# Loading wq by halves of its rows, summing Q in load order, two filler matmuls, and a new order table

## The chip, the cores and the metric

The kernel runs on one core of a Trainium2 chip. The metric is the device time of one execution in microseconds (us), the median of several runs. Before the change it is 269.3 us (four runs, 269.09 to 270.72).

## What is computed

The reference mixes two branches of the same input x (2048 tokens x 512, bf16), token by token, with a gate:

```python
x = A_x
g = sigmoid((x * gate_w).sum(-1, keepdims=True))
a = infini_attention(x, wq, wk, wv, wo, beta)        # 32 heads of 16
b = (relu(x @ W_gate) * (x @ W_up)) @ W_down          # 512 -> 1792 -> 512
return g * a + (1 - g) * b
# attention, for each of 4 segments of 512 tokens:
#   o = gb * (phi(q) @ M) / (phi(q) @ z) + (1 - gb) * causal_softmax(q k' / 4) v
#   M += phi(k)' v ;  z += sum(phi(k))               # phi(t) = t + 1 if t > 0 else exp(t)
```

## The kernel before, in words

**Tiling.** The 2048 tokens are four segments of 512 (L). x is kept transposed (xT, four chunks of 128 features by 512 tokens). Every projection is a set of matmuls of 128x128 weights by 512 tokens: Q and K in four chunks of eight heads per segment (proj_q, proj_k), V in four token tiles (proj_v), gate and up of the feed-forward part in 14 chunks each (ffn_tasks), and the output in token tiles of 128 that sum the down projection and wo into the same PSUM bank (out_tile). Scores are packed four heads to the array's rows ("row" groups of 8 matmuls, L625, and the diagonal ones of 32, L638), probabilities times V four to its columns ("col" groups of 32, two per unit of eight heads, L697). PSUM is eight banks of 512 columns (pool "ps"), shared by all.

**Other engines.** ACT does exp of the scores (L646, four banks at once), exp for phi (L535) and relu (L847). DVE empties banks (QT L555, ktr L571, hT L853), makes the two masked copies of K (KT L574), phi (pkT, pqT, L530 and L531), transposes and normalises the attention output (T L728, cfr L736 and L738, och L733, oT L709) and sums x times gate_w (L433, reads xn, the natural rows of x). GpSimd masks the probabilities (L675). SP issues nearly all DMAs, in program order: loads (L299), the transposing loads of xT for segments 1 to 3 (load_xT, L306), xn of segments 1 to 3 (load_xn, L309), the transposing copies of pkT into pK (L587), Vm (L610), coefficients (coefs, cdr), and the stores of the output (L878).

**The order of the work.** The kernel does not leave the order to a scheduler of the compiler. Each piece of work is a task with an engine, an assumed duration, a key, dependencies and buffers that it needs and frees (plan.add). Plan.run plays the tasks through: on each engine the ready task of lowest key goes next, subject to free banks and buffers; then instructions are emitted in the order of the start times so found. The table SHIFT adds an amount to the key of single tasks, by the number of the task. LANDS gives the assumed landing time of each initial load, in ns. SP is assumed busy with these loads until 31,500 ns, and a load of xn to take 520 ns of SP and to land 3,500 later; a pK copy takes 1,200 and 2,000. None of these assumptions is a measured time of the chip; they only set the order. A wrong assumption shows as a wait at run time.

**The start.** Four 128-token tiles of x come in by SP and ACT queues (xn), followed on SP by wq in two halves of 256 columns, wk, wv, the first pieces of W_gate and W_up, and the rest. Six matmuls on a zeroed tile (heat, L888) keep PE busy while x is awaited. PE transposes the four tiles of x into xT of segment 0 (x0_tasks, flip, L510), the copies out of PSUM go by DVE and ACT (L516). In proj_q of segment 0 the first two chunks (those that lie in the first half of wq) are computed in two halves of 256 tokens, each as a sum over the four feature chunks; the other two chunks in one piece of 512 tokens.

Tensors of one pool are told apart by a number: four pkT buffers hold phi(k) until pK has been copied from them, and a fifth write to pkT waits for the first copy to land.

```python
got_q = [load_cols(nc.sync, wq_sb, A_wq, 256 * i, 256 * i + 256, "q" + "ab"[i])
         for i in range(2)]
```

```python
plan.add("SP", 520, KA(4 * seg - 4), lambda seg=seg: load_xn(seg), att["xn", seg - 1], 3500)
```

Of the kernel before, what the change touches and what calls it, by code (L numbers as in the profile page):

```python
# [12 lines left out]
P = 128  # L13
# [6 lines left out]
L = S // NSEG  # L20
F = 1792
NC = D // P
# [7 lines left out]
RH = 14  # L30

SHIFT = {
    43: -11292, 47: -42077, 60: 29780, 61: -29343, 78: -7855, 80: -28982, 81: 10949, 82: 54730,
    83: 61225, 85: 1523, 92: 60668, 99: 17134, 105: 23333, 108: 6042, 135: 68788, 155: 81196,
    171: -26874, 178: 28954, 203: 14280, 206: 25983, 212: 15078, 215: -1330, 218: -18032,
    221: -5316, 224: -4814, 230: 4174, 233: -3831, 239: 5098, 242: 32097, 245: 1369, 248: 1978,
    254: 346, 257: -3395, 260: -10949, 263: -6816, 266: 12793, 272: -2789, 275: -11469,
    283: -20102, 284: 10561, 299: 13751, 337: 44621, 342: 12310, 345: 10169, 354: -30001,
    356: -45046, 358: 80101, 368: -61348, 372: -4345, 373: -49237, 380: -41791, 389: 27518,
    391: 4652, 394: -20195, 395: -41145, 400: 33640, 401: 12661, 405: 14171, 414: 8957,  # L40
    420: 65824, 446: -24413, 476: 42115, 512: 24141, 533: 21455, 550: -7924, 553: -9644,
    555: -16953, 562: 1704, 565: -3083, 574: 10306, 577: -6358, 583: -18575, 586: 1273,
    589: -14836, 592: -5785, 595: -12158, 598: -6986, 601: -6263, 604: -2900, 610: -5726,
    613: -20978, 619: 12853, 631: -124737, 670: 51001, 671: 27573, 677: -73050, 681: 4127,
    695: -9393, 700: 6645, 709: 12451, 714: -3470, 737: -44032, 739: 33239, 743: 5687,
    746: -27812, 761: 17624, 777: 24417, 789: 46875, 813: -11642, 829: 49888, 844: -14954,
    862: 32683, 867: -2735, 873: 4060, 879: 1169, 882: 518, 888: 10427, 891: -5165, 897: -3609,
    900: -8372, 903: -10859, 906: -5138, 912: -7446, 915: -6121, 924: 1808, 927: 3218, 930: 4603,
    942: 3963, 945: 1904, 948: -2731, 975: 7041, 987: 40475, 1007: -59044, 1014: 8606,
    1022: 31523, 1025: 4449, 1030: 2648, 1047: -2009, 1052: 10394, 1058: 20655, 1064: 9096,  # L50
    1067: 9109, 1099: -58805, 1134: 19973, 1151: -15341, 1161: -24899, 1162: -66525,
    1185: -54718, 1191: -19721, 1197: 30339, 1203: -5307, 1206: -13430, 1209: 25922,
    1218: -21029, 1224: 86677, 1230: 1511, 1236: -18972, 1239: -22798, 1242: -9229, 1245: 8841,
    1248: 7291, 1251: 33147, 1257: -26262, 1260: -16305, 1263: -14082,
}


# [154 lines left out]
def kernel(  # L212
# [15 lines left out]
    nc = tc.nc  # L228
# [7 lines left out]
    plan = Plan()  # L236

    def sb(shape, dtype, name):
        return wpool.tile(shape, dtype, name=name)
# [6 lines left out]
    xT = [sb([P, NC, L], BF16, f"xT{i}") for i in range(3)]  # L246
    xn = sb([P, 4, D], BF16, "xn")
    wq_sb = sb([P, NC, D], BF16, "wq_sb")
# [35 lines left out]
    def bank(slot):  # L284
        return ps[:, slot.i * L:(slot.i + 1) * L]

    def work():
        return plan.one("ps", range(7, -1, -1))


    LANDS = dict(n0=3500, n1=3700, n2=4750, n3=4850, qa=5600, qb=6900, k=8800, v=10200, g0=11700,
                 u0=13500, gw=14100, be=14200, g1=15700, u1=19000, x1=21200, g2=22400, u2=23700,
                 g3=24800, u3=25900, d0=28500, d1=31100, o=32700, x2=35700)

    def arrival(name):
        return plan.add("in_" + name, 0.0, 0.0, None, lat=LANDS[name])

    def load(eng, dst, src, name):
        eng.dma_start(out=dst, in_=src)  # L299
        return arrival(name)  # L300

    def load_cols(eng, t, ap, c0, c1, name):
        return load(eng, t[:, :, c0:c1], ap.rearrange("(c p) n -> p c n", p=P)[:, :, c0:c1], name)
# [9 lines left out]
    got_x, got_n, got_g, got_u = {}, {}, {}, {}  # L313
# [5 lines left out]
    def load_wd(a, b, name):  # L319
# [2 lines left out]

    got_n[0] = [load(nc.scalar if t % 2 else nc.sync, xn[:, t, :], x[t * P:(t + 1) * P, :],
                     "n%d" % t) for t in range(4)]
    got_q = [load_cols(nc.sync, wq_sb, A_wq, 256 * i, 256 * i + 256, "q" + "ab"[i])
             for i in range(2)]
    got_k = load_cols(nc.sync, wk_sb, A_wk, 0, D, "k")
    got_v = load_cols(nc.sync, wv_sb, A_wv, 0, D, "v")
# [8 lines left out]
    junk = sb([P, L], BF16, "junk")  # L337
# [80 lines left out]
    PEL, DVL, ACL, POL = 230, 150, 165, 130  # L418
    att, prj, ffn, xread, x0_first = {}, {}, {}, [], []
    UNIT, AUNIT = 16000.0, 14800.0  # L420

    def K(unit, part=0.0):
        return unit * UNIT + part
# [57 lines left out]
    def matmuls(key, deps, sl, ops, start=True, stop=True, prev=None, width=L, need=(), chunk={}, at=0):  # L481
        n = len(ops)
        for k in range(0, n, GM):
            def emit(k=k):
                for q in range(k, min(k + GM, n)):
                    lhsT, rhs = ops[q]()
                    nc.tensor.matmul(bank(sl)[:, at:at + width], lhsT=lhsT, rhs=rhs,  # L487
                                     start=(start and q == 0), stop=(stop and q == n - 1))
            first = prev is None
            m = min(k + GM, n) - k  # L490
            t = plan.add("PE", 215.8 * width / L * m, key - (0 if first else CONT), emit,
                         list(deps) + [d for q in range(k, k + m) for d in chunk.get(q, ())],
                         PEL, need=[sl] + list(need) if first else ())
            if not first:
                t.deps.append((prev, 0.0))
            prev, deps = t, ()
        return prev
# [4 lines left out]
    def x0_tasks():  # L502
        got = []
        parts = [(0, 0, 4), (1, 0, 4), (2, 0, 4), (3, 0, 2), (3, 2, 4)]
        for n, (t, c0, c1) in enumerate(parts):
            sl = work()

            def flip(t=t, c0=c0, c1=c1, sl=sl):
                for c in range(c0, c1):
                    nc.tensor.transpose(bank(sl).bitcast(BF16)[:, c * P:(c + 1) * P],  # L510
                                        xn[:, t, c * P:(c + 1) * P], ident[:])
            a = plan.add("PE", 107.0 * (c1 - c0), K(-9) + n, flip, [got_n[0][t]], PEL, need=[sl])
            act = n in (1, 4)
            b = plan.add(
                "ACT" if act else "DVE", 60 + (0.83 if act else 0.56) * P * (c1 - c0),
                K(-9), lambda t=t, c0=c0, c1=c1, sl=sl, act=act: (  # L516
                    nc.scalar.copy if act else nc.vector.tensor_copy)(
                    xT[0][:, c0:c1, t * P:(t + 1) * P],
                    bank(sl).bitcast(BF16)[:, c0 * P:c1 * P].rearrange("p (c q) -> p c q", q=P)),
                [a], DVL, frees=[sl])  # L520
            got.append(b)
        x0_first.extend(got[0:2])
        return [got[0:4], got[0:3] + got[4:5]]

    def proj_mm(w, c, seg):
        return [lambda ci=ci: (w[:, ci, c * P:(c + 1) * P], xT[seg % 3][:, ci, :])
                for ci in range(NC)]
# [10 lines left out]
    def proj_q(seg, c):  # L538
        u, sl = 4 * seg + c, work()
        i = u % RQ  # L540
        key = K(4 * seg + c - 2 - (2 if seg else 0))
        war = [att.get(("pv", u - RQ)), att.get(("recall", u - RQ))]
        if seg == 0 and c < 2:
            a = None
            for h in range(2):
                a = matmuls(key + 20000 * (h - 1), [got_q[0]], sl, [
                    lambda ci=ci, h=h: (wq_sb[:, ci, c * P:(c + 1) * P],
                                        xT[0][:, ci, h * L // 2:(h + 1) * L // 2])
                    for ci in range(NC)], width=L // 2, at=h * L // 2, prev=a,
                    chunk={ci: got_x[0][ci // 2] if h else x0_first for ci in range(NC)})  # L550
        else:
            a = matmuls(key, [got_q[c // 2]] + war, sl, proj_mm(wq_sb, c, seg),
                        chunk={ci: got_x[seg][ci // 2] for ci in range(NC)})
        xread.append(a)
        prj["q", seg, c] = plan.add("DVE", 600, key - RQK, lambda: nc.vector.tensor_copy(  # L555
            QT[i][:], bank(sl)), [a], DVL, frees=[sl])
        if seg:
            es, b = phi_exp(key, lambda: QT[i][:], prj["q", seg, c])
            prj["pq", seg, c] = plan.add("DVE", 665, key + 500, lambda: phi(
                pqT[i][:], QT[i][:], ex1[es.i][:]), [b], DVL, frees=[es],  # L560
                lock=True)
# [321 lines left out]
    GM, CONT, QKP, PVP = 2, 10000.0, 1e6, 1e5  # L883
# [73 lines left out]
```

## Time and profile before

| what | value |
|---|---|
| median of four runs | 269.3 us (269.09, 269.26, 269.35, 270.72) |
| the profiled execution | 269.09 us |
| its span (first to last instruction) | 267.4 us |
| instructions in the profile | 7193 |
| first matmul on wq | at 5.90 us |
| last eviction (osr, L875) | 264.36 to 264.84 us |
| mean DMA rate | 77 GB/s, 20.52 MB in 32567 packets |
| packets under 512 B, under 2 KB | 15000, 31000 |
| granted TensorE clock | 1.00 throughout |

All times in the profile are microseconds from the start of the span, of one execution. PE is TensorE's matmuls, PEld its weight loads, DVE VectorE, ACT ScalarE, POOL GpSimd; SPq is SP's queue, that is, the issuing of DMAs. "L487" is a line of the kernel: it is the line of the matmul in the helper `matmuls`, so all projections share it, and they are told apart by their tiles (ps<-xT,wq_sb is Q). A matmul's recorded duration includes its way through the array and is longer than the step from one matmul to the next; where steps matter, they are taken from start to start. The chain of waits is the work that ended last, followed back from the last instruction. A DMA's landing is the last of its completion increments in the trace.

### The profile page before, as it was taken

To read this page: it belongs to the slowest core of one execution; us is meant where nothing else is said; L and a number is where in the kernel's file an instruction comes from. 1 tells how busy PE (TensorE), PEld (TensorE's weight loads), DVE (VectorE), ACT (ScalarE), POOL (GpSimd) and SP (SyncE) were. 2 spreads that over 40 slices of the span, in tenths; PEclk is the share of its full clock that TensorE was granted. 3 is DMA by queue.
4 is the path that set the end of the run, shared out by engine and by line. 5 is a ranking of instruction groups with operands and counts; after the bars stand their busy time and mean duration, and the time that the engine had idled before them with its cause. 6 is when DMAs were issued, how large, how long until landed. Compare 5 with 4: busy or idle time off the path is not lost.

```text
span 267.4 us, 7193 instructions
## 1 busy us (share of the span) xinstructions
PE 262.5 (98%) x3022; PEld 117.3 (44%) x3022; DVE 197.9 (74%) x455; ACT 182.7 (68%) x168; POOL 57.8 (22%) x146
## 2 busy tenths in 40 slices
PE   7999999999999999999999999999999999999995
PEld 4544444444444444443444444344444444444444
DVE  3898889999997798899699287477996566554412
ACT  3299859999977779897897857745988656243200
POOL 7032112313222231322223222201132302200000
PEclk9999999999999999999999999999999999999999
DMA  7999972132626112011601210000310210000011
GB/s 208 341 263 338 266 167 41 23 99 50 112 52 182 31 37 91 2 20 42 116 19 25 88 54 9 2 0 2 81 55 2 93 56 20 2 0 2 0 39 39
DMA packets 32567, 20.52 MB, mean 77 GB/s; under 512 B 15000, under 2 KB 31000, under 8 KB 32536
## 3 DMA queue, kind: packets, MB, share of 16 engines
q1 hardware_dynamic: 32248, 19.82, 28.1%
q8 instruction: 23, 0.38, 0.7%
q10 hardware_dynamic: 288, 0.26, 0.4%
q14 instruction: 8, 0.07, 0.1%
HBM read 13.21 MB, written 2.55 MB: 59 GB/s over the span
## 4 chain that ended last, share of the span: by engine, by line
PE 95%; DMA 3%; DVE 1%; SPq 0%; issue 0%
PE ps L487 77%; PE ps L625 8%; PE ps L697 7%; DMA wq_sb<-in_A_wq_dram 2%; DMA pK<-pkT 1%; PE ps L783 1%; PE ps L638 1%; PE ps L802 1%; SPq L299 0%; DVE T L728 0%; PE ps L753 0%; DVE osr L875 0%; DVE pkT L530 0%; PE ps L452 0%; DVE pkT L531 0%
## 5 line engine op out<-in xcount | busy, mean ns | idle before, releaser
L646 ACT ACTIVATE E<-ps 128x2048 bf16<-128x2048 f32 x64 | 120.1, 1877 | 27.4 <-PE ps L625 21.5
L675 POOL TENSOR_SCALAR_AFFINE_SELECT E<-E 128x256 bf16<-128x256 bf16 x128 | 53.0, 438 | 172.0 <-ACT E L646 172.0
L487 PE MATMUL ps<-xT,wg_sb 128*128 128x512 bf16 x224 | 58.0, 380 | 0.0
L487 PE MATMUL ps<-xT,wu_sb 128*128 128x512 bf16 x224 | 56.5, 380 | 0.0
L487 PE MATMUL ps<-wd_sb,hT 128*128 128x512 bf16 (+1 forms) x238 | 55.3, 368 | 0.0
L853 DVE TENSOR_TENSOR hT<-ps,rgr 128x512 bf16<-128x512 f32 x56 | 37.7, 686 | 20.5 <-ACT rgr L847 11.6
L847 ACT ACTIVATE rgr<-ps 128x512 bf16<-128x512 f32 x56 | 32.9, 600 | 20.4 <-PE ps L487 20.4
L487 PEld LDWEIGHTS <-wu_sb 128*128 128x128 bf16 x224 | 21.0, 98 | 26.1 <-issue 2.6
L487 PEld LDWEIGHTS <-hT 128*128 128x128 bf16 x238 | 21.6, 98 | 24.2 <-issue 3.8
L487 PEld LDWEIGHTS <-wg_sb 128*128 128x128 bf16 x224 | 20.3, 98 | 25.0 <-issue 3.2
L875 DVE TENSOR_SCALAR osr<-ps,ngcol 128x512 bf16<-128x512 f32 (+1 forms) x17 | 12.0, 707 | 20.1 <-PE ps L487 20.1
L728 DVE STREAM_TRANSPOSE T<-ps 128x512 f32<-128x512 f32 x32 | 21.1, 696 | 7.2 <-PE ps L697 6.5
L625 PE MATMUL ps<-QT,KT 32*128 32x320 bf16 (+3 forms) x512 | 25.4, 273 | 0.0
L697 PE MATMUL ps<-E,Vp 128*17 128x320 bf16 (+3 forms) x512 | 18.8, 274 | 0.0
L646 ACT ACTIVATE Em<-ps 128x2048 bf16<-128x2048 f32 x8 | 15.0, 1874 | 4.6 <-PE ps L638 4.6
L625 PEld LDWEIGHTS <-KT 32*128 32x128 bf16 x512 | 7.7, 92 | 23.0 <-issue 22.1
L487 PE MATMUL ps<-xT,wk_sb 128*128 128x512 bf16 x64 | 17.0, 381 | 0.4 <-DVE T L728 0.4
L487 PE MATMUL ps<-wv_sb,xT 128*128 128x512 bf16 x64 | 17.0, 380 | 0.0
L487 PE MATMUL ps<-wo_sb,oT 128*128 128x512 bf16 (+1 forms) x68 | 16.6, 367 | 0.0
L487 PE MATMUL ps<-xT,wq_sb 128*128 128x512 bf16 (+1 forms) x72 | 16.5, 356 | 0.1
L697 PEld LDWEIGHTS <-Vp 128*17 128x17 bf16 x512 | 8.0, 91 | 10.0 <-issue 4.7
L571 DVE CAST ktr<-ps 128x512 bf16<-128x512 f32 x16 | 11.0, 686 | 1.6 <-PE ps L487 1.3
(87 smaller groups left out, 231.9 us busy)
## 6 DMA issues: line engine op xcount, KB each, us to landing
cdr<-coefs SPq DMA_DIRECT2D x12, 256.0 KB
out_dram<-osr SPq DMA_DIRECT2D x15, 128.0 KB
wd_sb<-in_B_W_down_dram SPq DMA_DIRECT2D x2, 896.0 KB
xn<-in_A_x_dram SPq DMA_DIRECT2D x3, 512.0 KB
Vm<-Vp SPq DMA_DIRECT2D x8, 144.0 KB
wg_sb<-in_B_W_gate_dram SPq DMA_DIRECT2D x2, 512.0 KB
wu_sb<-in_B_W_up_dram SPq DMA_DIRECT2D x2, 512.0 KB
wg_sb<-in_B_W_gate_dram SPq DMA_DIRECT2D x2, 384.0 KB
```

Of the source, the lines that this page charges most:

```text
L487: nc.tensor.matmul(bank(sl)[:, at:at + width], lhsT=lhsT, rhs=rhs, start=(start and q == 0), stop=(stop and q == n - 1))
L571: d = plan.add("DVE", 600, key - RQK, lambda: nc.vector.tensor_copy(ktr[ks.i][:], bank(sl)), [a], DVL + 40, need=[ks], frees=[sl])
L625: nc.tensor.matmul(ps[:, j * L + o:j * L + o + L - q], lhsT=KT[i][rows, kb, 3 * r:3 * r + 2].rearrange("p h q -> p (h q)"), rhs=QT[i][rows ...
L638: nc.tensor.matmul(ps[:, o:o + HP], lhsT=KT[i][rows, kb, 2:4].rearrange("p h q -> p (h q)"), rhs=QT[i][rows, kb * P:kb * P + HP], start=Tr ...
L646: last_exp[0] = [plan.add("ACT", 66 + 4 * L / 1.2, key, lambda: nc.scalar.activation(dst, ps[:, 0:4 * L], ACT.Exp, scale=SCALE), [a] + war ...
L675: nc.gpsimd.affine_select(out=m[:, :, o:o + HP], in_=m[:, :, o:o + HP], compare_op=ALU.is_ge, fill=0.0, base=HP, pattern=[[0, 4], [1, HP]] ...
L697: nc.tensor.matmul(bank(sl)[32 * j:32 * j + HW, q:q + w], lhsT=(Vp[i] if n < 4 else Vm)[:, kb, r, 4 * c + j, 0:HW], rhs=rhs, start=(n == 0 ...
L728: done.append(plan.add("DVE", 633, key - RL, lambda r=r, sl=sl: nc.vector.transpose(T[ts.i][:, r], bank(sl)), [a] + done, 75 if r else 0, ...
L783: a = plan.add("PE", 216, key, lambda: nc.tensor.matmul(bank(sl), lhsT=mbd[i][:, c].rearrange("p j r e -> p (j r e)"), rhs=pqT[u % RQ][:], ...
L847: r = plan.add("ACT", 478, key - RL, lambda sl=gsl, rs=rs: nc.scalar.activation(rgr[rs.i][:], bank(sl), ACT.Relu), [g], ACL, frees=[gsl])
L853: nc.vector.tensor_tensor(hT[hs1.i][:], bank(sl), rgr[rs.i][:], ALU.mult)),
L875: b = plan.add("DVE", 95 + 1.12 * w, key - RL, lambda: nc.vector.tensor_scalar(osr[os.i][:, 0:w], bank(sl)[:, 0:w], ngcol[:, tt:tt + 1], N ...
```

## The change

Four edits. First, wq is loaded in two halves of its rows (feature chunks 0 and 1, then 2 and 3, all 512 columns) instead of two halves of its columns. Second, Q of segment 0 is summed in the order in which these arrive, for all four chunks: the first 256 tokens over feature chunks 0 and 1, the second 256 tokens over chunks 0 and 1, then all 512 tokens over chunks 2 and 3; the three parts are sums into the same bank. Third, two matmuls of 256 columns on the zeroed tile are put after the transposes of the second tile of x and after those of the last. Fourth, LANDS has new values and SHIFT is another table: some 150 entries before, an entry for nearly every task after; the numbers of the tasks change as well, since Q has more tasks. With that the order of instructions on PE, DVE, ACT and SP changes everywhere except in stretches. The counts of instructions stay the same but for the two filler matmuls (with their weight loads). In the new order xn of segment 1 stands second after Vm on SP, behind the first pK copy (before: third, behind two), and on DVE the first operation that reads it (L433) stands right behind the first two T transposes of segment 0.

```diff
 SHIFT = {
-    43: -11292, 47: -42077, 60: 29780, 61: -29343, 78: -7855, 80: -28982, 81: 10949, 82: 54730,
...
+    23: 127287, 24: 109748, 25: 61282, 26: -14683, 27: -105670, 28: 80312, 29: 20669, 31: 93713,
...
-    LANDS = dict(n0=3500, n1=3700, n2=4750, n3=4850, qa=5600, qb=6900, k=8800, v=10200, g0=11700,
-                 u0=13500, gw=14100, be=14200, g1=15700, u1=19000, x1=21200, g2=22400, u2=23700,
-                 g3=24800, u3=25900, d0=28500, d1=31100, o=32700, x2=35700)
+    LANDS = dict(n0=3500, n1=3700, n2=4750, n3=4850, qa=5750, qb=6500, k=8050, v=9550, g0=11100,
+                 u0=12900, gw=13500, be=13600, g1=15100, u1=18400, x1=20600, g2=21800, u2=23100,
+                 g3=24200, u3=25300, d0=27900, d1=30500, o=32100, x2=35100)
...
-    got_q = [load_cols(nc.sync, wq_sb, A_wq, 256 * i, 256 * i + 256, "q" + "ab"[i])
+    got_q = [load(nc.sync, wq_sb[:, 2 * i:2 * i + 2],
+                  A_wq.rearrange("(c p) n -> p c n", p=P)[:, 2 * i:2 * i + 2], "q" + "ab"[i])
              for i in range(2)]
...
             a = plan.add("PE", 107.0 * (c1 - c0), K(-9) + n, flip, [got_n[0][t]], PEL, need=[sl])
+            if n in (1, 4):
+                fs = work()
+                plan.add("PE", 213 if n == 1 else 110, K(-9) + n + 0.5, lambda fs=fs:
+                         nc.tensor.matmul(bank(fs)[:, 0:2 * P], lhsT=junk[:, 0:P],
+                                          rhs=junk[:, None, 0:P].to_broadcast([P, 2, P]),
+                                          start=True, stop=True), [(a, 0.0)], PEL, need=[fs], frees=[fs])
...
-        if seg == 0 and c < 2:
+        if seg == 0:
             a = None
-            for h in range(2):
-                a = matmuls(key + 20000 * (h - 1), [got_q[0]], sl, [
-                    lambda ci=ci, h=h: (wq_sb[:, ci, c * P:(c + 1) * P],
-                                        xT[0][:, ci, h * L // 2:(h + 1) * L // 2])
-                    for ci in range(NC)], width=L // 2, at=h * L // 2, prev=a,
-                    chunk={ci: got_x[0][ci // 2] if h else x0_first for ci in range(NC)})
+            parts = [(0, L // 2, 0, x0_first), (L // 2, L, 0, got_x[0][0]), (0, L, 2, got_x[0][1])]
+            for n, (l0, l1, c0, got) in enumerate(parts):
+                a = matmuls(key + 20000 * (n - 2) + CONT * (n > 0), [], sl, [
+                    lambda ci=ci, l0=l0, l1=l1: (wq_sb[:, ci, c * P:(c + 1) * P],
+                                                 xT[0][:, ci, l0:l1])
+                    for ci in (c0, c0 + 1)], start=(n == 0), stop=(n == 2), width=l1 - l0, at=l0,
+                    prev=a, chunk={0: got + [got_q[c0 // 2]]})
         else:
-            a = matmuls(key, [got_q[c // 2]] + war, sl, proj_mm(wq_sb, c, seg),
+            a = matmuls(key, list(got_q) + war, sl, proj_mm(wq_sb, c, seg),
                         chunk={ci: got_x[seg][ci // 2] for ci in range(NC)})
```

## The prediction

> **What bounds the kernel now.** I read the page's engine rows first, then the chain of waits, then the table of stretches, then the timeline of DVE and of SP's queue around the one place where TensorE stands still.
>
> ```profile
> PE 262.5 (98%) x3022; PEld 117.3 (44%) x3022; DVE 197.9 (74%) x455; ACT 182.7 (68%) x168; POOL 57.8 (22%) x146
> ```
>
> PE is busy all but 5 us of the span. The chain (start, length, what) says where those 5 us are:
>
> ```profile
> 1.75 4.11 DMA wq_sb<-in_A_wq_dram
> 5.90 6.67 PE ps L487 x38
> ...
> 32.79 3.14 DMA pK<-pkT
> 35.95 0.31 DVE pkT L530
> 36.31 0.31 issue
> 36.62 0.72 DVE T L728
> 37.38 1.45 PE ps L487 x6
> ...
> 264.36 0.48 DVE osr L875
> ```
>
> Three things are to be seen. The first Q matmul (5.90) is released by the first half of wq (landed at 5.85). After that the chain is PE, line after line, until 264.3; then one eviction and one store end the span. Only once does it leave PE: a transposing DMA of pK, issued by SP at 32.79, releases DVE's pkT write (it needs that pkT buffer back), the two T transposes queue behind it on DVE, and PE waits for the bank that the first T frees. Start to start, PE loses 0.60 us there (36.77 to 37.38). Elsewhere after 5.9 I find 0.10 at 25.1, 0.14 at 68.5 and 0.14 at 168.0, and a few hundredths.
>
> DVE is the next engine (us, then busy PE, PEld, DVE, ACT, POOL):
>
> ```profile
> 6.00:38.00 32.00, 31.57 (x285) 14.24 (x285) 27.05 (x73) 23.24 (x27) 6.64 (x14) 1.00 1.01 277
> 38.00:100.00 62.00, 61.97 (x840) 26.77 (x839) 56.71 (x143) 52.00 (x46) 16.54 (x40) 1.00 0.33 77
> ```
>
> From 38 to 100 us DVE has 5.3 us free in 62. Until 38 us the DMA engines are busy all the time (share 1.01).
>
> ```profile
> 23.80 7.39 SPq L306 DMA_TRANSPOSE xT<-in_A_x_dram  x1
> 31.32 1.37 SPq L610 DMA_DIRECT2D Vm<-Vp  x2
> 32.79 3.23 SPq L587 DMA_TRANSPOSE pK<-pkT  x2
> 36.12 0.54 SPq L309 DMA_DIRECT2D xn<-in_A_x_dram  x1
> 36.62 1.31 DVE L728 STREAM_TRANSPOSE T<-ps 128x512 f32<-128x512 f32 x2
> 38.46 0.68 DVE L571 CAST ktr<-ps 128x512 bf16<-128x512 f32 x1
> 40.72 0.68 DVE L433 SCALAR_TENSOR_TENSOR junk<-xn,gwb 128x512 bf16<-128x512 bf16 x1
> ```
>
> SP is held by the transposing load of segment 2's xT for 7.39 us, so all that stands behind it in SP's order is late. By the trace's completion records the first pK landed at 35.93, the second at 37.31, xn (the natural rows of segment 1, for the gate) at 40.30. DVE first reads xn at 40.72, just after.
>
> **What the Trainium skill says.** "TensorE: Matmul & The Clock Gate", section "Wait — 56ns, not 53.3ns?": start to start a warm matmul takes N / 2.4 GHz and about 2.5 ns; cold, N / 1.2 GHz. The trace agrees: 216 ns at 512 columns, 109 at 256; the transposes step by 107 ns until 4.57 and by 55 from 4.98, so the clock is already full at the first Q. "DMA: Bandwidth & Descriptors", section "Specifications": 512 B is the least piece for full rate. Column halves of wq have 512 B pieces, row halves 1 KB; so little is to be won, and the trace agrees: wq's second half (256 KB) lands 0.79 us after the first, 332 GB/s, against 512 KB of wv in 1.50 us, 350 GB/s. Same page, section "Queues, rings and completion order": on each DMA engine descriptors are consumed in the order of the ring. That bears on xn behind pK; the landings above are in order of issue.
>
> **The change, part by part.**
>
> *Row halves of wq, Q in load order.* Same bytes, same 72 wq matmuls (16 of 256 columns). From the rates above a half saves 256 KB / 332 GB/s - 256 KB / 350 GB/s = 0.04 us. The first Q starts at 5.9, perhaps 5.75: gain 0 to 0.15. In the built order PE needs the second half after 12 x 0.109 = 1.3 us (it lands 0.79 after the first) and wk after 2.39 us (12 + 2 of 0.109 and 4 of 0.216), that is at 8.29; wk landed at 8.11. wv is needed at 9.80, landed 9.61; gate's second piece at 15.41 (before: 24.5), landed 15.14. All margins are thin (0.1 to 0.3) but positive: 0, at worst 0.3 of stall.
>
> *Two fillers.* 0.109 us each warm, 0.213 cold. The first stands where PE is idle from 4.63 to 4.98 waiting for x, the second where it is idle from 5.62 to 5.90 waiting for wq. Both covered; if wq came early, the second would show 0.11.
>
> *None of that reaches the end.* The wait at 37.38 is set by SP and the DMA (7.39 us of xT, Vm, pK landing 35.93), not by PE. In the changed order SP's first four of these are the same, and so are DVE's pkT, T, T. Summing PE's matmuls with the durations above (score group 0.33 and 0.10 to enter it, PV pair 1.22), from the first Q to the matmul that waits for T both orders give 30.75 us. So a gain of 0.15, or a stall of up to 0.6, before 36.8 vanishes in this wait. Value taken: 0, the ends -0.1 (if the loads come earlier by two halves) and +0.1.
>
> *The new order (SHIFT, LANDS).* This is the larger part: almost every task's key changes. Three counts from the built orders. (1) Entries from full-array matmuls into score or PV groups: 79 before, 77 after, 0.098 us each (62 of them measured): -0.19. (2) Waits of PE on DVE or ACT whose releasing work begins with a matmul less than 1.55 us before: 23 before and 23 after (past 37 us). So close waits are as many; the small stalls (0.14, 0.14) I carry over unchanged, with -0.3 and +0.4 as ends. (3) Loads: from 76 to 98 us the two orders are nearly the same; near 68 the gate's small loads come earlier.
>
> One place differs for the worse. In SP's new order xn stands right behind the first pK, and in DVE's new order the first gate operation (L433, reads xn) stands right behind the two T, ahead of the cast of K (ktr); before, the cast came at once (38.46), the gate at 40.72. Working it out: SP is free for xn at 34.76 (32.79 and the first pK's issue, 1.93 by the trace). The one xn issued into an almost empty queue (54.03) landed 3.61 us later: 38.36 at the earliest. In this stretch xn landed 2.99 after the pK ahead of it (37.31 to 40.30): 35.93 + 2.99 = 38.92 at the latest by that row. I take 38.7. DVE ends T at 37.93 and waits to 38.75; the gate's pair takes 0.72, the cast 0.68, the signal 0.06: PE has the bank at 40.2. PE wants it 2.16 us after 37.38 (in the new order four wk, two wq, a score group with its entry, two wq: 8 x 0.216 + 0.43), at 39.54. Stall 0.67 (0.33 to 0.9). Queued behind on DVE: cfr, four KT, och, oT, then QT0, hT. By the same sums QT0 is ready at 43.2 (wanted at 43.3), the second hT at 45.0 (wanted at 44.9): another 0.15. DVE's later gate operations are the same number, so what is done early here is not owed later, but PE's loss is not given back: PE has no idle time.
>
> *Sum against the profiled execution* (269.09 us, its span 267.4 and 1.7 outside): 269.09 + 0.67 + 0.15 - 0.19 = 269.72. The median of the runs, 269.3, lies 0.2 above that execution: **269.9**.
>
> *Tail.* The last two tiles change places, but the last piece is a 256-column half as before: 18 x 0.109, eviction 0.48, store to the end. 0.
>
> **The rivals.**
> *Nothing new is late* (the order is as good as the old, xn in time): only the 0.19 counts, and perhaps the two 0.14: 269.3 - 0.2 - 0.1 = 269.0. For it: 23 close waits against 23. Against: DVE reaches the gate at 37.93, and no xn in the trace landed less than 3.6 us after issue. That halving by rows changes nothing measurable by itself is part of this case and of mine.
> *Slower: xn lands late.* In a busy queue xn took 5.63 us (80.65 to 86.29). Issued at 34.76 it would land at 40.4, the cast would end at 41.9, PE would stand 2.3 us at 39.54: 269.3 + 2.3 + 0.15 - 0.19 = 271.6. For it: xT's and Vm's packets fill the queue until 35, DVE has little spare time until 100 us. Against: at 80.65 it stood behind two slow spreads of coefs (the cdr loads) that are not there at 35. It decides slower from a landing at 39.4 on (stall 1.4).
>
> **Numbers.** What counts as faster or slower is 0.5%, about what a measurement of this kernel can tell from no change: below 267.95 or above 270.65. Faster is hardly in reach: all of PE's stalls after 5.9 are 1.0 us, the switches 0.2, and 0.6 of the stalls is set by SP. Chances: forecast 0.48 (269.3 to 270.5), nothing late 0.27 (268.7 to 269.3; below 267.95 only if the counts miss something, 0.04), xn late 0.25 (270.7 to 271.6). Faster 0.04, same 0.70, slower 0.26. The range runs from 268.7 to 271.5.
>
> **What would show it.** First Q at 5.75 to 5.9, fillers with no wait behind them, wk matmul near 8.2. The wait for T again near 37.4. DVE's first gate operation with idle time before it released by the DMA of xn, PE with a wait of 0.3 to 0.9 for the ktr cast near 39.5. PE's entries into groups: 77. Wrong if xn lands by 38.0, if the T wait moves with the first Q, or if PE waits over 1 us in sum past 46 us.

## The result and the profile after

| | before | after |
|---|---|---|
| median | 269.86 us (55 runs, 269.02 to 271.19) | 271.02 us (34 runs, 269.94 to 273.49) |
| ratio after / before | | 1.0050, 95% interval 1.0036 to 1.0064 |
| profiled execution | 269.09 us, span 267.4 | 271.78 us, span 270.1 |

The change makes the kernel 1.2 us (medians) to 1.35 us (ratio) slower. The two profiled executions lie 2.7 us apart, more than the medians: the one of before is a quick one of its kind, the one of after a late one. So no single difference between the two traces is read as a cost below until runs confirm it.

The engine row and the waits of PE (engine, line waited for: us in total, times, longest), of after:

```profile
PE 262.9 (97%) x3024; PEld 117.3 (43%) x3024; DVE 197.6 (73%) x455; ACT 182.9 (68%) x168; POOL 59.9 (22%) x146
```

```profile
PE ps L1012 <- DVE mcol_e L471: 1.1, 1, 1.1
PE ps L604 <- DVE ktr L695: 0.9, 1, 0.9
PE ps L821 <- DVE omr L912: 0.6, 1, 0.6
PE ps L604 <- DVE T L852: 0.5, 1, 0.5
PE ps L604 <- DMA wq_sb<-in_A_wq_dram: 0.4, 1, 0.4
PE ps L604 <- DVE osr L999: 0.2, 1, 0.2
PE ps L604 <- DVE hT L977: 0.2, 1, 0.2
```

Lines have moved by 117 to 124 (L487 is now L604, ktr L571 is L695, T L728 is L852, the gate operation L433 is L550, omr L788 is L912). omr is the attention recalled from memory times the coefficients cdr, osr the output on its way to the store, hT the feed-forward product. The same view of before has, past the start, one line: 0.4 for T. New are ktr, omr, osr and hT (wq is the start). The timeline of after from 24 to 46 us:

```profile
24.77 6.94 SPq L422 DMA_TRANSPOSE xT<-in_A_x_dram  x1
31.90 1.38 SPq L734 DMA_DIRECT2D Vm<-Vp  x2
33.32 1.88 SPq L711 DMA_TRANSPOSE pK<-pkT  x1
35.30 0.53 SPq L425 DMA_DIRECT2D xn<-in_A_x_dram  x1
37.12 1.31 DVE L852 STREAM_TRANSPOSE T<-ps 128x512 f32<-128x512 f32 x2
37.88 1.02 PE L604 MATMUL ps<-xT,wk_sb 128*128 128x512 bf16 x4 [0.53 <-DVE T L852]
39.70 0.69 DVE L550 SCALAR_TENSOR_TENSOR junk<-xn,gwb 128x512 bf16<-128x512 bf16 x1 [1.27 <-DMA xn<-in_A_x_dram]
40.32 0.69 DVE L695 CAST ktr<-ps 128x512 bf16<-128x512 f32 x1
41.06 1.02 PE L604 MATMUL ps<-xT,wg_sb 128*128 128x512 bf16 x4 [0.85 <-DVE ktr L695]
...
45.94 1.02 PE L604 MATMUL ps<-xT,wk_sb 128*128 128x512 bf16 x4 [0.15 <-DVE hT L977]
```

To be seen: DVE ends T at 38.43 and stands 1.27 us until xn has landed (39.68); the ktr cast, whose matmuls end at 38.90, follows the gate operation, and PE gets its bank at 41.06. The chain of waits of after goes through a second place, which the chain of before did not have:

```profile
99.91 2.47 DMA coefs<-dnr
...
103.07 5.04 DMA cdr<-coefs
108.11 0.03 issue
...
108.20 0.70 DVE omr L912
108.90 0.04 issue
108.94 0.73 PE ps L821 x32
```

DVE's omr waits for a cdr that landed at 108.11, and PE for omr. In before it is PE that the operation waits for last, and PE loses nothing behind it:

```profile
100.01 1.26 SPq L780 DMA_DIRECT2D cdr<-coefs  x2
103.90 0.69 DVE L788 TENSOR_TENSOR omr<-ps,cdr 128x512 bf16<-128x512 f32 x1 [0.38 <-PE ps L783]
```

**A ledger.** To add such things up I took, in every trace, the start of each 128x128 matmul minus the time it would have if every matmul took its start-to-start step (the durations of the prediction). Jumps of this difference are PE's losses (in us, at the times of after):

| place | before | after |
|---|---|---|
| groups of PV and T, 36 to 38 us | 0.59 | 0.30 + 0.69 |
| ktr at 41.06, hT at 45.94 | 0.09 | 1.02 + 0.21 |
| T, osr, hT, 93 to 103 us | 0 | 0.64 |
| omr, 107 to 110 us | 0 | 0.75 |
| others over 0.06 | 0.28 | 0.25 |

Without its losses PE's work from the first Q on is 0.2 us shorter in after (257.0 against 257.2).

### The profile page after: what moved, and what is told of

Same layout as the page of the kernel before. It is cut to its first block, busy times and chain, and to the rows that moved or that the text cites. A ratio compares the mean times of both kernels' runs of the same rounds, so it can differ in the third digit from the quotient of the medians.

```text
span 270.1 us, 7202 instructions
## 1 busy us (share of the span) xinstructions
PE 262.9 (97%) x3024; PEld 117.3 (43%) x3024; DVE 197.6 (73%) x455; ACT 182.9 (68%) x168; POOL 59.9 (22%) x146
## 4 chain that ended last, share of the span: by engine, by line
PE 71%; SPq 13%; DMA 8%; DVE 6%; issue 1%; ACT 1%; DVEq 0%
PE ps L604 58%; PE ps L749 5%; PE ps L821 5%; SPq L422 5%; SPq L415 5%; DMA ratio<-rcol 2%; DMA cdr<-coefs 2%; DMA xn<-in_A_x_dram 2%; DVE junk L550 1%; DMA coefs<-dnr 1%; PE ps L762 1%; PE ps L907 1%; DMA rq<-ratio 1%; ACT Em L770 1%; SPq L711 1%
## 5 line engine op out<-in xcount | busy, mean ns | idle before, releaser
L799 POOL TENSOR_SCALAR_AFFINE_SELECT E<-E 128x256 bf16<-128x256 bf16 x128 | 55.2, 454 | 171.4 <-ACT E L770 171.4
L604 PE MATMUL ps<-xT,wg_sb 128*128 128x512 bf16 x224 | 57.6, 380 | 0.9 <-DVE ktr L695 0.9
L604 PE MATMUL ps<-xT,wu_sb 128*128 128x512 bf16 x224 | 56.8, 380 | 0.3 <-DVE osr L999 0.2
L604 PE MATMUL ps<-wd_sb,hT 128*128 128x512 bf16 (+1 forms) x238 | 54.6, 367 | 0.0
L604 PEld LDWEIGHTS <-hT 128*128 128x128 bf16 x238 | 22.0, 98 | 24.2 <-issue 2.7
L604 PEld LDWEIGHTS <-wg_sb 128*128 128x128 bf16 x224 | 20.8, 98 | 26.7 <-issue 3.5
L604 PEld LDWEIGHTS <-wu_sb 128*128 128x128 bf16 x224 | 20.6, 98 | 26.1 <-issue 3.7
L852 DVE STREAM_TRANSPOSE T<-ps 128x512 f32<-128x512 f32 x32 | 21.2, 697 | 5.8 <-PE ps L821 5.7
L604 PE MATMUL ps<-xT,wq_sb 128*128 128x512 bf16 (+1 forms) x72 | 17.7, 357 | 0.4 <-DMA wq_sb<-in_A_wq_dram 0.4
L604 PE MATMUL ps<-wv_sb,xT 128*128 128x512 bf16 x64 | 17.6, 380 | 0.0
L604 PE MATMUL ps<-xT,wk_sb 128*128 128x512 bf16 x64 | 16.9, 379 | 0.7 <-DVE T L852 0.5
L604 PE MATMUL ps<-wo_sb,oT 128*128 128x512 bf16 (+1 forms) x68 | 17.0, 368 | 0.0
L679 DVE CAST QT<-ps 128x512 bf16<-128x512 f32 x16 | 10.8, 681 | 4.5 <-PE ps L604 4.4
L912 DVE TENSOR_TENSOR omr<-ps,cdr 128x512 bf16<-128x512 f32 x12 | 8.1, 684 | 8.1 <-PE ps L907 6.1
```

Of the source, the lines that this page charges most:

```text
L799: nc.gpsimd.affine_select(out=m[:, :, o:o + HP], in_=m[:, :, o:o + HP], compare_op=ALU.is_ge, fill=0.0, base=HP, pattern=[[0, 4], [1, HP]] ...
L852: done.append(plan.add("DVE", 633, key - RL, lambda r=r, sl=sl: nc.vector.transpose(T[ts.i][:, r], bank(sl)), [a] + done, 75 if r else 0, ...
```

## Experiments

All but c and d are edits of the order in which tasks are emitted, between `order = plan.run()` and the loop that emits them (f and h add such an edit to c and d); `after(t, mark)` takes a task out of the order and puts it behind another one. c adds matmuls, and d changes loads and sums. None leaves work out. A ratio is to the kernel before, run on the same chip, with its 95% interval; medians of before lay between 269.79 and 269.86. Runs are called by their first letters below.

| run | median us | ratio to before |
|---|---|---|
| a_gate_back | 270.21 | 1.0015 (0.9996 to 1.0033) |
| b_gate_front | 270.69 | 1.0024 (1.0011 to 1.0038) |
| c_late_start | 270.05 | 1.0006 (0.9990 to 1.0022) |
| d_halves_old_order | 269.62 | 0.9999 (0.9976 to 1.0021) |
| e_xt_late | 268.96 | 0.9959 (0.9944 to 0.9974) |
| f_xt_late_start_late | 269.35 | 0.9987 (0.9966 to 1.0008) |
| h_xt_late_halves | 269.28 | 0.9987 (0.9971 to 1.0002) |
| g_pk_back | 269.79 | 1.0011 (0.9996 to 1.0026) |
| k_pk_back_only | 270.27 | 1.0019 (1.0007 to 1.0030) |
| l_pk_front | 269.82 | 1.0021 (0.9995 to 1.0047) |
| i_mended_xt_late | 269.56 | 0.9996 (0.9983 to 1.0009) |
| m_coefs_early | 269.01 | 0.9973 (0.9960 to 0.9987) |

### The gate operation in front of the cast

**a_gate_back** takes it out of the kernel after:

```diff
+    after(att["xn", 1][0], prj["q", 1, 0])
```

> The changed kernel with one instruction moved: DVE's first gate operation of segment 1 (the first that reads xn) goes back behind the cast of the first Q chunk (QT). Theory (DVE waits for xn ahead of the ktr cast, PE pays 1.02 us at 41.06 and 0.21 at 45.94): PE's wait for ktr is gone, the kernel is 1.0 us faster than the changed one (0.7 to 1.3), near 270.0 in the median. Rival (the lateness is spread over the new order, and the next close wait takes what this one gives back): no change, within 0.2 us of the changed kernel.

**b_gate_front** puts it, with its load, into the kernel before:

```diff
+    first = [t for t in order if t.eng == "SP" and t.dur == 1200][0]
+    after(got_n[1][0], first)
+    after(att["xn", 1][0], att["tt", 0])
```

> The kernel before with the mechanism alone: xn of segment 1 is issued right behind the first pK copy, ahead of the second, and DVE's first gate operation stands right behind the first two T transposes, ahead of the ktr cast. Nothing else changes. Theory: DVE stands idle for xn (landing 38.7 to 39.7), PE waits 0.7 to 1.1 us for the ktr cast, and the kernel is 0.7 to 1.1 us slower than before. Rival (this pair is not what costs; the whole order is): within 0.2 us of before.

a is 0.81 us faster than after by the medians, 0.94 by the ratios (1.0050 - 1.0015); its trace has no loss at ktr or hT. b is 0.85 slower than before by the medians, 0.65 by the ratio. Its timeline shows the mechanism alone:

```profile
39.82 0.69 DVE L433 SCALAR_TENSOR_TENSOR junk<-xn,gwb 128x512 bf16<-128x512 bf16 x1 [1.34 <-DMA xn<-in_A_x_dram]
...
40.93 0.69 DVE L571 CAST ktr<-ps 128x512 bf16<-128x512 f32 x1
...
41.67 1.02 PE L487 MATMUL ps<-xT,wu_sb 128*128 128x512 bf16 x4 [0.55 <-DVE ktr L571]
```

Taken out it gives back what put in it costs, in two different orders: the gate operation in front of the cast is the cause of 0.65 to 0.95 us. (a moves the operation alone and leaves the load of xn early, so it is the operation's place that costs.) The rival (lateness spread over the order) falls for this part. a remains 0.4 us above before, with an interval that just includes zero.

### What sets the wait for T, and does it take in the start

**c_late_start** adds, in the kernel before, four matmuls on the zeroed tile behind the last transpose of x:

```diff
+                for k in range(4 if n == 4 else 0):
+                    nc.tensor.matmul(ps[:, k * L:(k + 1) * L], lhsT=junk[:, 0:P],
+                                     rhs=junk[:, None, 0:P].to_broadcast([P, 4, P]), start=True,
+                                     stop=True)
```

> The kernel before with four more filler matmuls of 512 columns after the last transpose of x, which delay the first Q by about 0.58 us. Theory (the wait for T at 37.38 is set by SP and the DMA, and takes in anything up to 0.6 that comes before it): the first Q starts near 6.5, PE's stall of 0.60 at 37.4 shrinks to about 0, the time is within 0.15 us of before. Rival (the start is on the path to the end): 0.58 us slower.

**d_halves_old_order** is the announced change in the old order: row halves, load-order sums for the first two chunks, both fillers, no new table.

```diff
-    got_q = [load_cols(nc.sync, wq_sb, A_wq, 256 * i, 256 * i + 256, "q" + "ab"[i])
+    got_q = [load(nc.sync, wq_sb[:, 2 * i:2 * i + 2],
+                  A_wq.rearrange("(c p) n -> p c n", p=P)[:, 2 * i:2 * i + 2], "q" + "ab"[i])
...
+                if n in (1, 4):
+                    nc.tensor.matmul(ps[:, 0:2 * P], lhsT=junk[:, 0:P],
+                                     rhs=junk[:, None, 0:P].to_broadcast([P, 2, P]), start=True,
+                                     stop=True)
...
+            pieces = [(0, 2, 0), (0, 2, L // 2), (2, 3, None), (3, 4, None)]
```

> The kernel before with its own order of instructions, but wq loaded in row halves, Q of the first two chunks of segment 0 summed in load order, and the two fillers: the change without its new order table. Theory (halves and fillers are covered or vanish in the wait for T): within 0.15 us of before. Rival (the halves or fillers themselves cost, for example by a later second half or wk): 0.3 to 1 us slower, with PE waits between 5.9 and 12 us.

Both stay within 0.25 us of before by the medians, with intervals that reach 0.6 us: the first Q began at 7.09 us in the trace of c, at 5.54 in that of d. But in c the stall for T did not shrink to nothing as I had expected (it is 0.62), for the wait had moved too. In c:

```profile
34.01 3.23 SPq L591 DMA_TRANSPOSE pK<-pkT  x2
...
37.84 1.31 DVE L732 STREAM_TRANSPOSE T<-ps 128x512 f32<-128x512 f32 x2
...
38.60 1.02 PE L487 MATMUL ps<-xT,wk_sb 128*128 128x512 bf16 x4 [0.46 <-DVE T L732]
```

In each trace where PE waits here it goes on a fixed time after the first pK has landed, and that lands a fixed time after wo, the last of the weights:

| trace | wo landed | first pK landed | PE goes on |
|---|---|---|---|
| before | 31.44 | 35.93 | 37.38 |
| after | 31.96 | 36.42 | 37.88 |
| b_gate_front | 31.99 | 36.48 | 37.93 |
| c_late_start | 32.66 | 37.14 | 38.60 |
| d_halves_old_order | 31.71 | 36.18 | 37.63 |
| l_pk_front (below) | 31.90 | 36.38 | 37.84 |

4.46 to 4.49 us, then 1.45 to 1.46. So the loads set this wait, and they differ by up to 1.2 us between these executions. The first expectation was right in its mechanism and wrong in taking the landing of one trace for a constant.

**e_xt_late** moves the load that holds SP, in the kernel before, behind the fifth pK copy; **f** and **h** do the same in c and d:

```diff
-    load_xT(2)
+    pass
...
+    copies = [t for t in order if t.eng == "SP" and t.dur == 1200]
     for t in order:
         if t.emit is not None:
             t.emit()
+        if t is copies[4]:
+            load_xT(2)
```

> The kernel before with one instruction of SP moved: the transposing load of segment 2's xT, which held SP for 7.39 us ahead of Vm and the pK copies, is issued behind the fifth pK copy instead (near 41 us; it is first read near 67). Theory (the first pK copy sets the wait for T, and SP's hold at a full queue sets that copy): the first pK lands before 34, PE's stall of 0.60 at 37.4 is gone, the load itself now holds SP about 2 us as segment 3's does, and the kernel is 0.5 to 0.7 us faster than before. Rival (the next release is just as late, or the load disturbs xn and pK at 41 to 50): within 0.2 us.

> The run with the four 512-column fillers (c_late_start) with the same move of the transposing load. Theory: with the wait for T gone nothing takes in the late start any more, so it counts in full: slower than e_xt_late by the delay of the first Q (about 1.1 us by the trace of c_late_start, 7.09 against 5.90), that is 0.4 to 0.7 us slower than before, although c_late_start itself was within 0.2 us of before. Rival (the start never mattered, or always did): the same distance from e_xt_late as c_late_start had from before (0.2 us).

> Row halves, load-order sums and fillers in the old order (d_halves_old_order), with the transposing load moved in the same way. Theory: what the halves win at the start (0.1 to 0.35 us of the first Q) now reaches the end: 0.1 to 0.35 us faster than e_xt_late, 0.6 to 1.0 us faster than before. Rival (the halves win nothing): equal to e_xt_late.

e is 0.85 us faster than before by the medians, 1.1 by the ratio. SP's queue in e, and PE where it waited for T:

```profile
24.56 2.05 SPq L610 DMA_DIRECT2D Vm<-Vp  x2
26.71 4.00 SPq L587 DMA_TRANSPOSE pK<-pkT  x2
30.81 0.53 SPq L309 DMA_DIRECT2D xn<-in_A_x_dram  x1
31.44 5.92 SPq L587 DMA_TRANSPOSE pK<-pkT  x3
37.41 1.92 SPq L306 DMA_TRANSPOSE xT<-in_A_x_dram  x1
```

```profile
36.82 1.02 PE L487 MATMUL ps<-xT,wk_sb 128*128 128x512 bf16 x4
```

No wait is marked at this matmul any more; the first pK landed at 33.65 though wo landed at 32.37, and the load itself takes 1.92 us of SP in place of 7.39. By the ledger 0.11 us is lost here, where before, after, b, c, d and l lose 0.59 to 1.16 (waits for Vm just ahead counted in), so the gain has the size of this wait.

f is 0.39 slower than e by the medians, 0.75 by the ratios, which fits a late start that counts once the wait is gone; but these intervals can't tell it from the 0.2 by which c is behind before, and f's trace loses 0.6 more at 92 to 107 besides the 0.49 of its first Q. Against before f is 0.46 faster and not slower, as I had written: its first Q came at 6.29, not at 7.09 as in the trace of c (the four fillers step by 216 ns in f, and the first two by 427 in c), and e had won more than 0.6.

h did not do what I expected: 0.3 slower than e and not faster. In its trace the first Q began at 5.85 but ran its first five steps at 188 to 214 ns in place of 109 (0.5 us lost), where e's stepped by 110 from the second on. Whether halves and fillers tend to delay the clock, or one trace caught a late one, these runs don't tell: full clock came between 4.0 and 7.0 us in the eight traces with them, and between 4.5 and 6.8 in the six without.

### The rest of the new order

Ratio and rq carry the gate's factors through DRAM to the layout that the attention output needs; DVE's product with rq (grc) stands ahead of other work of DVE, the next T among it. In a, PE loses 2.1 us at 92 to 103 us and 0.25 at 107. At 92 to 103 DVE waits for rq, which follows ratio, which was issued behind cdr and xn; the new order issues a pK copy ahead of these. In a (DVE, and the waits of PE):

```profile
90.03 0.38 DVE L590 TENSOR_TENSOR grc<-rq,gcat 128x128 f32<-128x128 f32 x1 [1.25 <-DMA rq<-ratio]
```

```profile
PE ps L604 <- DVE T L852: 1.2, 1, 1.2
```

**g_pk_back** (on a) and **k_pk_back_only** (on after) put it behind rtok; **l_pk_front** moves the like copy in the kernel before the other way:

```diff
+    sp = [t for t in order if t.eng == "SP"]
+    k = min(sp.index(prj["pk", 2, c]) for c in range(NC))
+    after(sp[k], sp[k + 6])     # l: after(sp[k], sp[k + 1])
```

> The changed kernel with the gate operation moved back (a_gate_back) and one SP instruction more: the pK copy that the new order issues at 78 us, ahead of cdr, xn and ratio, goes behind rtok, 7 places later. Theory (this copy's 4 us in the queue make ratio and so rq land 0.6 to 1.4 us later against PE than before, and DVE, which waits for rq, lets PE stand at 94 to 102): the stalls of PE between 92 and 103 (2.1 us in the trace of a_gate_back) fall under 0.5, and the kernel is 0.4 to 1.0 us faster than a_gate_back. Rival (ratio is late for the slow spreads of cdr themselves, which stand in front of it in both orders): within 0.2 us of a_gate_back.

> The changed kernel with only the pK copy of 78 us moved behind rtok on SP; the gate operation stays in front. Theory (two separate losses: the gate's, 1.2 us at 41 to 46, and the copy's, at 94 to 110): the stalls at 41 to 46 stay, those at 94 to 103 (0.6 us in the changed kernel's trace) go, and the kernel is 0.3 to 1.0 us faster than the changed one, 270.0 to 270.7. Rival (the copy is innocent and the stalls of 94 to 103 come with the spread of the cdr landings from run to run): within 0.2 us of the changed kernel, stalls at 94 to 103 of 0.5 us or more.

> The kernel before with one SP instruction moved: its pK copy of 73.92 us goes behind coefs, so that it stands right ahead of the store and the cdr spreads, as in the new order. Theory (the copy in front of cdr, xn and ratio makes rq late): rq lands 0.4 to 1.0 us later against PE than in before, PE stands 0.3 to 1.0 us at 94 to 103, and the kernel is 0.2 to 0.9 us slower than before. Rival (the place of the copy doesn't matter): within 0.2 us of before, no stall above 0.3 at 94 to 103.

The times: g 0.42 faster than a by the medians but 0.1 by the ratios, which is within the noise; k 0.75 faster than after; l as before by the medians, 0.2% slower by a ratio whose interval includes 1. The traces: no loss at 92 to 103 in g, 0.63 in k (as in after), none in l. So the stall is not tied to the copy's place. What it goes with, over these traces, is rq's landing; no run moved rq alone. Less PE's own lateness up to there (the ledger), rq landed at 87.4 to 87.9 in before, b, c, d, l and g, without loss; at 88.2 in after and k, with 0.6 lost; at 89.1 in a, with 2.1. In a it was coefs, ahead of all these on SP, that came late: it took 4.65 us from issue to landing, and 2.46 to 2.56 in the other traces. The old order is near the edge as well: f crossed it (88.5, 0.8 lost), h too (88.2, 0.25). e doesn't fit: it lost 0.24 at 87.4. k's gain in time is larger than what its trace explains; the copy's share stays open.

At 107 it is different: the loss for omr is in all five traces of the new order up to here (after 0.75, a 0.25, g 0.50, k 0.50, i 0.60) and in none of before, b, c, d and l (e, f and h lose 0.2 to 0.3 there, for hT and not for omr). The two loads of cdr that follow the second coefs store land 1.4 to 1.9 us one after the other in these five traces. In the new order the omr at this place waits for the semaphore of the second of them, in the old order for that of the first: it begins at 108.20 in after, with the second landed at 108.11 and the first already at 106.35; in l at 104.58, with the first landed at 104.49 and the second not before 105.95. In all five traces of the new order it begins 0.08 to 0.10 us behind the second. The first is read only at 129.54 in after. So the table has turned the order of the two loads against the order of their use. I had not seen that when I wrote the next expectation, which blames the store ahead of them (it leaves about 0.5 us later against PE than in before).

**i_mended_xt_late** is after with the moves of a, g and e; **m_coefs_early** adds, on i:

```diff
+    den, co = att["den", 1, 1], att["coefs", 1, 1]
+    after(den, [t for t in order[:order.index(den)] if t.eng == "DVE" and t.dur == 835][-1])
+    sp = [t for t in order if t.eng == "SP"]
+    after(co, max(den, sp[sp.index(co) - 3], key=order.index))
```

> The changed kernel with all three moves: the gate operation behind the first QT cast, the pK copy behind rtok, and the transposing load of segment 2's xT behind the fifth pK copy. Theory (the new order is 0.19 us better by its entries, and its losses are these three places): as fast as e_xt_late (268.96) or up to 0.3 us faster. Rival (the new order has further close waits that now come out): 0.3 to 0.8 us slower than e_xt_late.

> The mended new order (i_mended_xt_late) with one more pair moved: on DVE the product that makes the second set of coefs of segment 1 stands right behind its reciprocal (before osr and hT, not after), and on SP that coefs store goes ahead of the output store and rq. Theory (in the new order this store leaves about 0.5 us later against PE than before, cdr lands at 105.5 to 106, DVE's omr waits for it, and PE stands 0.5 to 0.6 at 106.5 in every trace of the new order): cdr lands 1.3 to 1.8 us earlier, DVE's omr no longer waits for cdr, PE's stall near 107 falls from 0.60 to under 0.15, and the kernel is 0.3 to 0.5 us faster than i_mended_xt_late, 269.1 to 269.3. Rival (PE's stall there is set by something else that omr only happens to precede): the stall stays, within 0.15 us of i_mended_xt_late.

i is 0.6 us slower than e (0.37% by the ratios), as its rival said. Not all of that need be the table: i has the halves and fillers too, h with these in the old order is itself 0.3 slower than e, and i and h can't be told apart (0.9996 and 0.9987). DVE and PE in i:

```profile
105.96 0.69 DVE L912 TENSOR_TENSOR omr<-ps,cdr 128x512 bf16<-128x512 f32 x1 [0.92 <-DMA cdr<-coefs]
```

```profile
106.70 0.61 PE L821 MATMUL ps<-E,Vp 128*17 128x448 bf16 x16 [0.43 <-DVE omr L912]
```

and SP, DVE and PE in m:

```profile
96.20 0.54 SPq L896 DMA_DIRECT2D coefs<-dnr  x1
97.18 0.34 SPq L1002 DMA_DIRECT2D out_dram<-osr  x1
```

```profile
105.15 0.68 DVE L912 TENSOR_TENSOR omr<-ps,cdr 128x512 bf16<-128x512 f32 x1
```

```profile
106.28 0.61 PE L821 MATMUL ps<-E,Vp 128*17 128x448 bf16 x16
```

```profile
97.19 1.02 PE L604 MATMUL ps<-xT,wu_sb 128*128 128x512 bf16 x4 [0.61 <-DVE osr L999]
```

The store leaves 1.8 us earlier than in i (97.96), the second cdr lands at 104.56 and not at 105.86, omr waits for nothing and the loss at 107 is gone: the chain from coefs over cdr to omr is its cause. That the turned pair alone would do it is argued from the landings; changing the two loads back wasn't tried. In this trace 0.77 is lost again at 97.19, where osr now stands behind the product. The median is 0.55 better than i's, while of the trace of m against that of i 0.55 is the first Q (with the slow first steps of i), -0.60 the place at 107 and +0.77 that at 97. So the place is shown; what it is worth in the median is not.

The best kernels are e (268.96) and m (269.01), 0.8 to 0.9 us under before and 2.0 to 2.1 under after by the medians; e needs one moved instruction.

## Why the prediction was right or wrong

**The start** (row halves, load-order sums, fillers: 0). Right, as far as d can tell (0.9999, with 0.6 us to either side). First Q at 5.92, fillers at 4.32 and 5.26 with PE idle 0.38 behind the second. The margin of wk, "at worst 0.3 of stall", was passed in a: wk landed at 8.67 and PE lost 0.38. It was taken in later, for a has no wait for T.

**"None of that reaches the end".** Right in mechanism (c, e, and the fixed 1.45 us behind pK's landing), and with a size that was missing: pK's landing is not 35.93 but 35.5 (k) to 37.1 (c) by execution. In after's trace it was 0.49 later, a term that the sum did not have.

**The main step** (gate operation behind T, ahead of ktr: 0.67 + 0.15). Right in mechanism and place, and in the median right in size: 0.82 predicted, 0.81 (a) and 0.85 (b) measured by the medians, 0.94 and 0.65 by the ratios. In the trace of after it is larger, 1.02 + 0.21: xn landed 3.26 us behind the first pK (3.31 in b, 3.05 in k), where I had taken 2.77, below the row of 2.99 that the trace showed. xn's landing of 39.68 lies past the 39.4 that I gave as the rival's point, but PE itself was 0.5 late by then, so the stall was 1.0 and not the 1.65 that the same sum gives for 39.68: the forecast's mechanism at a size between the two cases.

**The rest of the order** (-0.19, "close waits are as many; the small stalls (0.14, 0.14) I carry over unchanged"). This is the step that failed, in its second half. The -0.19 came true: 77 entries into groups in every trace of the new order, and 0.2 us less of PE's work. What failed is that the waits were put at no change. Past 46 us the ledger has 0.28 us of losses in before, b, c, d and l (0.74 to 1.31 in e, f and h), and 0.70 to 2.52 in after, a, g, k, i and m. Without the gate operation in front the new order is 0.4 us slower than before (a, with an interval that just includes zero), not 0.2 faster. The part that is shown is omr's, 0.25 to 0.75 in each trace until m mends it; that at 92 to 103, 0 to 2.1, stays open. I counted waits of PE on DVE and ACT that follow closely on a matmul, and compared the loads only from 76 to 98 us. The two cdr loads that have changed places are issued at 102.40 and 103.07. A close wait counted as one looked the same whether DVE's operation reads the first or the second of them. By my own mark (over 1 us of PE's waits past 46) the forecast is wrong there: the trace of after has 1.57 by the ledger, though the list of waits alone shows 0.8.

**The median** (269.3 from four runs). 55 runs gave 269.86. Of the 1.1 us between 269.9 and 271.02 about 0.55 is this, and about 0.55, reckoned from the median of a, the failed step. So 271.02 lies in the band that I had given to the rival of a late xn (270.7 to 271.6) and not in that of the forecast (269.3 to 270.5), and that it lies inside the range at all is partly luck: by the medians the gate operation cost what I had forecast, and a base taken too low and the waits past 46 us made up the rest.

## What to carry to other kernels

When an instruction is moved ahead of another on an in-order engine, ask for its latest input, not its length: a gate operation of 0.69 us cost 0.8 us because its load was still in flight while the cast behind it was ready. For loads that come in pairs, compare the order of issue with the order of use: turned round, a pair can delay its reader by the distance of its landings (1.4 to 1.9 us here, of which PE lost 0.25 to 0.75), and my count of close waits did not show it. And before a start is trimmed, find the next wait that is set by transfers: here the place of one transposing load, issued while weights were still in flight, took in what a start won or lost and was itself worth 0.85 us.

## What the runs showed of the hardware

The same kind of transposing load (512 tokens by 512) held SP for 6.6 to 7.6 us where weights were still in flight ahead of it, and for 1.9 to 2.1 us later, when they had landed; a pK copy held it 1.2 us near 75 us in before, and 3.25 and 3.76 us in g and k, where it stands behind cdr and xn.

The full TensorE clock came at 4.0 us (m), 4.2 (after), 4.6 (before, where the table ahead of the prediction says throughout), 5.3 (d) and as late as 7.0 (h, i), though PE's first matmul starts at 1.05 or 1.06 in all. The Trainium skill, "TensorE: Matmul & The Clock Gate", Part 1 on the HAM clock gate, says that the activity window is free-running, so that the moment differs from run to run, by 500 ns to either side. The traces agree that it differs, but over 3.0 us, and 0.4 to 0.5 us of the first Q's steps hangs on it (g, h, i).

Landings need not follow the order of issue: in e ratio, issued at 80.22, landed at 85.86, ahead of a cdr spread (79.04 to 87.11) and xn (79.72 to 87.85). The skill's "DMA: Bandwidth & Descriptors", section "Queues, rings and completion order", says that completion is not first in, first out per issuing engine; the trace agrees, and my prediction had leant on the order of the landings of one trace.
